# Attention keys in chunks of 128, 128, 128 and 64 instead of 4 x 112, with the rests of scores and values on four quarters of TensorE

## The chip, the cores and the metric

The kernel runs on one core of a Trainium2 chip. The metric is the device time of one launch in microseconds (us). All quoted profiles and all comparisons are of fast runs. A difference of under 2% counts as "same"; where the study needs finer distinctions, the 95% interval of the ratio is given.

## The reference

Eight sequences with twelve heads of 448 tokens and 64 features go through attention with normalised queries and keys; its result, 3584 tokens of 768 features, goes through a normalised feed-forward layer.

```python
B, H, S, D = 8, 12, 448, 64
q_n, k_n = rmsnorm(q, g_q), rmsnorm(k, g_k)
scores = q_n @ k_n.T / sqrt(D)
attn = exp(scores - max) ; attn = attn / (sum(attn) + 1e-9)
x = (attn @ v)  ->  (B*S, H*D)
xn = x / sqrt(mean(x*x) + 1e-6) * rms_g                # 3584 x 768
out = (silu(xn @ w_gate) * (xn @ w_val)) @ w_out       # 768 -> 1536 -> 768
```

The weights arrive as float64 and are turned into fp32 on the chip.

## The kernel before

Heads are worked on in pairs, 48 of them (6 for each sequence). The loop runs over g; iteration g computes the scores of pair g, the values and sums of pair g - 1, and transposes the queries and keys of pair g + 1. The first seven iterations have no feed-forward work to mix in; from then on the feed-forward layer of the sequence before fills TensorE between the attention blocks. With 64 features a head needs half of the array's rows for its scores and half of its columns for its values, so the two heads of a pair run side by side.

Transposed scores: keys on the partitions, 448 queries along the free dimension; four chunks of 112 keys.

```python
def score(g, cs):                       # cs: chunks of keys
    for c in cs:
        for j in range(2):              # the two heads: two row halves of the array
            r = slice(j * D, (j + 1) * D)
            ps = sc[c, j] = ps_s.tile([128, 512], F32, name="sc", tag="s")
            nc.tensor.matmul(ps[0:P, 0:S], lhsT=qkT[r, 1, c * P:(c + 1) * P], rhs=qkT[r, 0, :], start=True, stop=True)
    for (c, j), ps in sc.items():
        e = st["e", g, c, j] = e_pool.tile([P, S], F32, name="e")
        nc.scalar.activation(e, ps[0:P, 0:S], ACT.Exp, scale=rs[:, n:n + 1])
    # ... GpSimd adds the e of one head up into es (late pairs)

def values(g):
    av = st["av", g] = ps_m.tile([128, 512], F32, name="av", tag="m")       # ps_m has one buffer
    for c in range(NT):
        for j in range(2):              # the two heads: two column halves of the array
            nc.tensor.matmul(av[j * D:(j + 1) * D, 0:S], lhsT=vt[:, j, c, :], rhs=st["e", g, c, j],
                             start=(c == 0), stop=(c == NT - 1))

def sums(g):
    # ones times es (late pairs: 2 matmuls) or times every e (the first pairs, "direct": 8 matmuls) -> den
    # rd = 1 / den on VectorE (after a copy on ScalarE in late pairs)
    nc.vector.tensor_tensor(x, av[:, 0:S], rd, ALU.mult)        # frees the bank of av
```

The loop body of the early and of the late iterations (squares, loads and feed-forward calls cut):

```python
if g <= NPAIR:                          # early
    pe(lambda: score(g, (0, 1)))
    ...
    pe(lambda: turn(g + 1, 0)); pe(lambda: turn(g + 1, 1))      # transposes of q and k
    pe(lambda: values(g - 1)); pe(lambda: sums(g - 1))
    pe(lambda: score(g, (2, 3)))
else:                                   # late
    pe(lambda: score(g, (0, 1)))
    pe(lambda: values(g - 1)); pe(lambda: sums(g - 1))
    pe(lambda: score(g, (2, 3)))
    ...                                 # feed-forward work, transposes
```

The conversion of the float64 weights is a pipeline of turns, called a few times an iteration. It shares ScalarE, VectorE and GpSimd with the attention:

```python
def convert():                          # turn n
    if 0 <= n - 4 < len(pieces):        # GpSimd: the last add; frees the raw buffer of piece n - 4
        nc.gpsimd.tensor_tensor(data(key).bitcast(I32), top, lo, ALU.add)
    if 0 <= n - 3 < len(pieces):        # VectorE: three operations
        st["cv", n - 3] = join(*st.pop(("cv", n - 3)))
    if 0 <= n - 2 < len(pieces):        # ScalarE: two operations, the first to read the raw weights
        st["cv", n - 2] = split(st.pop(("raw", n - 2)))
    if n < len(pieces):                 # SyncE: load of piece n, 384 KB, into one of six buffers
        st["raw", n] = load_raw(pieces[n][1])
    if 0 <= n - 6 < len(pieces):
        keep(pieces[n - 6][0])          # SyncE: store of the converted piece
```

## Time and profile before

| | kernel before |
|---|---|
| time, median of 4 runs beside the changed kernel | 1628.51 us (1628.03 to 1629.68) |
| profiled run | 1627.08 us, span 1625.3 us, granted clock 0.999 |
| TensorE, VectorE, ScalarE busy | 99%, 54%, 31% |
| one late pair's attention, start to start | 7.31 us |
| one early pair | 11.32 us |

TensorE is the bound nearly from end to end. The lines that carry this are in the prediction below. In profile lines, L476 and the like are lines of the kernel: before, `sc` is scores, `av` values, `den` sums, `tr` transposes and `ff` the feed-forward layer, all on TensorE (PE).

### The profile page before, as it was taken

The numbers are of one execution on the slowest core, as the hardware profiler recorded it, in microseconds if no ns is written. First come the engines' busy times: TensorE is split into PE (matmuls) and PEld (weight loads), VectorE is DVE, ScalarE is ACT, GpSimd is POOL, SyncE is SP. The second block draws the span as 40 slices with busy tenths as digits, with TensorE's granted clock in tenths as the row PEclk, the third lists the DMA queues.
The fourth block names the chain that finished last, engine by engine and source line by source line (L and its number), as shares of the span: only waits on it lengthen the run. The fifth ranks groups of instructions, "written<-read, shape, count | busy, mean of one in ns | idle before, by whom it ended". The sixth has DMA issues, their size and how long they took to land.

```text
span 1625.3 us, 21571 instructions
## 1 busy us (share of the span) xinstructions
PE 1608.9 (99%) x7376; PEld 1139.7 (70%) x7376; DVE 871.2 (54%) x1425; ACT 500.3 (31%) x975; POOL 632.2 (39%) x569
## 2 busy tenths in 40 slices
PE   8999999999999999999999999999999999999998
PEld 4444445678855888568865788658786588969974
DVE  6989898487842555335572354624565234433431
ACT  7856563232222332232232222322332123100110
POOL 7777776343523434244334323434343223100000
PEclk9999999999999999999999999999999999999999
DMA  8756674666855555565544655466454453557651
GB/s 223 208 176 200 183 219 134 217 222 200 267 183 154 164 154 156 166 197 154 155 120 131 201 155 147 120 215 194 130 163 132 147 176 108 152 182 239 175 148 45
DMA packets 249036, 276.83 MB, mean 170 GB/s; under 512 B 66644, under 2 KB 245844, under 8 KB 248916
## 3 DMA queue, kind: packets, MB, share of 16 engines
q1 hardware_dynamic: 248596, 275.34, 56.7%
q8 instruction: 61, 1.00, 0.3%
q14 instruction: 59, 0.48, 0.1%
q10 hardware_dynamic: 320, 0.00, 0.0%
HBM read 235.93 MB, written 39.32 MB: 169 GB/s over the span
## 4 chain that ended last, share of the span: by engine, by line
PE 91%; DVE 5%; DMA 2%; ACT 1%; issue 0%; POOL 0%; SPq 0%; DVEq 0%; ACTq 0%; POOLq 0%
PE ff L797 41%; PE ff L991 21%; PE sc L476 9%; PE av L501 9%; PE den L512 3%; PE ff L892 3%; PE ff L1022 2%; PE tr L461 2%; DVE top L646 1%; DVE top L645 1%; DVE rd L520 1%; DVE top L644 1%; DMA raw<-in_moe_w_out_dram 0%; ACT e L480 0%; PE rb L558 0%; DMA raw<-in_moe_w_val_dram 0%
## 5 line engine op out<-in xcount | busy, mean ns | idle before, releaser
L797 PE MATMUL ff<-x,w 128*128 128x224 f32 x1770 | 359.3, 353 | 0.8 <-DVE u L809 0.8
L797 PEld LDWEIGHTS ff<-x,w 128*128 128x128 f32 x1770 | 332.2, 190 | 9.8 <-issue 6.7
L797 PE MATMUL ff<-xs,w 128*128 128x224 f32 x1326 | 272.3, 353 | 0.4 <-DVE cc L809 0.4
L480 ACT ACTIVATE e<-sc,rs 112x448 f32<-112x448 f32 x384 | 212.1, 638 | 190.2 <-PE sc L476 185.2
L486 POOL TENSOR_TENSOR es<-e 112x448 f32<-112x448 f32 x82 | 95.3, 1184 | 436.1 <-ACT e L480 436.0
L797 PEld LDWEIGHTS ff<-xs,w 128*128 128x128 f32 x1326 | 248.6, 190 | 6.1 <-issue 5.3
L490 POOL TENSOR_TENSOR es<-es,e 112x448 f32<-112x448 f32 x164 | 185.9, 1144 | 85.4 <-ACT e L480 78.9
L991 PE MATMUL ff<-w,h 128*128 128x384 f32 x600 | 203.4, 488 | 0.0
L520 DVE RECIPROCAL rd<-rd 128x448 f32<-128x448 f32 x41 | 121.1, 2953 | 135.9 <-ACT rd L519 135.9
L476 PE MATMUL sc<-qkT 64*112 64x448 f32 x768 | 176.7, 562 | 1.6 <-DVE qkT L466 0.8
L991 PEld LDWEIGHTS ff<-w,h 128*128 128x128 f32 x600 | 112.3, 190 | 78.6 <-issue 4.7
L501 PE MATMUL av<-e,vt 112*64 112x448 f32 x768 | 154.9, 545 | 0.0
L444 POOL TENSOR_TENSOR rs<-ms,mhalf 112x16 f32<-112x16 f32 (+1 forms) x50 | 143.7, 2874 | 4.2
L476 PEld LDWEIGHTS sc<-qkT 64*112 64x112 f32 x768 | 68.8, 172 | 93.2 <-issue 69.5
L991 PE MATMUL ff<-w,so 128*128 128x384 f32 x338 | 116.7, 488 | 2.0 <-DVE y L952 2.0
L501 PEld LDWEIGHTS av<-e,vt 112*64 112x64 f32 x768 | 50.8, 136 | 95.8 <-issue 73.9
L1022 PE MATMUL ff<-x,w 128*128 128x448 f32 x288 | 112.0, 542 | 0.0
L809 DVE TENSOR_TENSOR cc<-ff,u 128x448 f32<-128x448 f32 x84 | 52.3, 623 | 93.3 <-PE ff L797 93.0
L991 PEld LDWEIGHTS ff<-w,so 128*128 128x128 f32 x338 | 63.2, 190 | 46.5 <-DVE y L952 3.9
L427 DVE TENSOR_REDUCE ms<-sq 112x8 f32<-112x512 f32 x96 | 61.3, 678 | 52.0 <-ACT sq L424 51.7
L682 POOL TENSOR_TENSOR w<-top,raw 128x384 int32<-128x384 int32 x72 | 78.0, 1097 | 28.3 <-DVE top L646 13.4
L1022 PEld LDWEIGHTS ff<-x,w 128*128 128x128 f32 x288 | 53.3, 190 | 50.9 <-issue 49.0
(104 smaller groups left out, 1676.2 us busy)
## 6 DMA issues: line engine op xcount, KB each, us to landing
w<-kept SPq DMA_DIRECT2D x480, 192.0 KB, 3.2
w<-kept_o SPq DMA_DIRECT2D x290, 192.0 KB, 2.8
kept<-w SPq DMA_DIRECT2D x94, 192.0 KB, 3.7
top<-kept SPq DMA_DIRECT2D x72, 192.0 KB, 3.0
qk<-in_q_dram SPq DMA_DIRECT2D x48, 224.0 KB, 3.6
qk<-in_k_dram SPq DMA_DIRECT2D x96, 112.0 KB, 3.5
vt<-in_v_dram SPq DMA_DIRECT2D x48, 224.0 KB, 2.8
raw<-in_moe_w_gate_dram SPq DMA_DIRECT2D x24, 384.0 KB, 4.7
```

Of the source, the lines that this page charges most:

```text
L427: nc.vector.tensor_reduce(out=ms[:, i * n:(i + 1) * n], in_=sq.rearrange("p (n d) -> p n d", d=D), axis=AX_X, op=ALU.add)
L444: nc.gpsimd.tensor_tensor(st["rs", g][:, cols], ms, mhalf[0:P, cols], ALU.pow)
L476: nc.tensor.matmul(ps[0:P, 0:S], lhsT=qkT[r, 1, c * P:(c + 1) * P], rhs=qkT[r, 0, :], start=True, stop=True)
L480: nc.scalar.activation(e, ps[0:P, 0:S], ACT.Exp, scale=rs[:, n:n + 1])
L486: nc.gpsimd.tensor_tensor(es, st["e", g, 0, j], st["e", g, 1, j], ALU.add)
L490: nc.gpsimd.tensor_tensor(es, es, st["e", g, c, j], ALU.add)
L501: nc.tensor.matmul(av[j * D:(j + 1) * D, 0:S], lhsT=vt[:, j, c, :], rhs=st["e", g, c, j], start=(c == 0), stop=(c == NT - 1))
L520: nc.vector.reciprocal(rd, rd)
L682: nc.gpsimd.tensor_tensor(data(key).bitcast(I32), top, lo, ALU.add)
L797: nc.tensor.matmul(bank[:, w * HT:(w + 1) * HT], lhsT=wt[:, c * 128:(c + 1) * 128], rhs=x[:, c, :], start=onto is None and w == c == 0, st ...
L991: nc.tensor.matmul(ps, lhsT=a, rhs=data(("wo", b, name, c)), start=first and c == 0, stop=c == NFP - 1, skip_group_check=True)
L1022: nc.tensor.matmul(bank[w][:, 0:S], lhsT=data(key)[:, c * 128:(c + 1) * 128], rhs=st["x", 0, half][:, c, :], start=half == c == 0, stop=ha ...
```

## The change

Its intent: 448 is three and a half times 128. With chunks of 112 keys the array's 128 columns (scores) or rows (values) are used to seven eighths, four times. With 3 x 128 + 64, three slots are full; the rest of 64 keys needs only a quarter of the array for each matmul (64 rows, 64 columns), so two heads' score rests (the two diagonal quarters) and two heads' value rests of the pair before (the other two) could run in one slot. For that the features of the two heads trade places in x (`place(j)`), and the feed-forward weights' rows are loaded in the matching order. The core of the diff:

```diff
-        for h in range(2):
-            nc.sync.dma_start(out=qk[:, 1]...[:, h], in_=k[b, 2 * hp + h]...)        # and q in one transfer
+        nc.sync.dma_start(out=to[:, :, 0:NK * D], in_=q[b, hs, full]...)             # 6 transfers a pair in place of 3
+        nc.sync.dma_start(out=to[0:REST, :, NK * D:], in_=q[b, hs, rest]...)         # 32 KB
+        for h in range(2):
+            nc.sync.dma_start(out=to[:, h, 0:NK], in_=k[b, 2 * hp + h, full]...)
+        nc.sync.dma_start(out=to[0:REST, :, NK], in_=k[b, hs, rest]...)              # 32 KB
+        nc.sync.dma_start(out=to[REST:128, 0, NK], in_=k[b, 2 * hp + 1, rest])       # 16 KB
 # values: 3 transfers in place of 1
+    def place(j):
+        return slice((1 - j) * D, (2 - j) * D)
+    def rests(g):
+        part = [slice(j * REST, (j + 1) * REST) for j in range(2)]
+        for r in part:                                          # scores of pair g, diagonal quarters
+            nc.tensor.matmul(ps[r, 0:S], lhsT=qkT[r, 1, NK * 128:S], rhs=qkT[r, 0, :], ...)
+        av = st["av", g - 1] = ps_m.tile([128, 512], F32, name="av", tag="m")
+        for j, r in enumerate(part):                            # values of pair g - 1, the other two quarters
+            nc.tensor.matmul(av[place(j), 0:S], lhsT=vt[r, 2 * NK * D:], rhs=e[r, :], start=True, stop=False, ...)
+        if direct(g - 1):                                       # early pairs: rests of the sums as well
+            ...
+        nc.scalar.activation(e, ps[:, 0:S], ACT.Exp, ...)       # one exponential for both heads' rests
 # the loop, early and late
-            pe(lambda: score(g, (0, 1)))
+        pe(lambda: (rests(g), score(g, (0,)) if g < NG else None))
 ...
-            pe(lambda: score(g, (2, 3)))
+            pe(lambda: score(g, (1, 2)))
 # raw weights: two pieces at a time, three double buffers for six single ones
-    raw_pool, cv_pool = pool("c_raw", 6), pool("c_cv", 4)
+    raw_pool, cv_pool = pool("c_raw", 3), pool("c_cv", 4)
-        if n < len(pieces):
-            st["raw", n] = load_raw(pieces[n][1])
+        if n < len(pieces) and n % 2 == 0:
+            load_raw(n)
```

Why the weights are paired: the swapped rows make a gate or value piece two transfers (64 partitions each). Pairing two pieces keeps the number of transfers as it was. Cut: the memsets of the padding, 128 for 112 in normalisation and transposes, and the output's rows.

## The prediction

> **What bounds the kernel now.** I read the engine table first, then the stretch table (busy time of each engine in chosen windows), then the time line of TensorE in one late pair and in one early pair, and last the chain of waits at the start.
>
> ```profile
> PE 1608.9 (99%) x7376; PEld 1139.7 (70%) x7376; DVE 871.2 (54%) x1425; ACT 500.3 (31%) x975; POOL 632.2 (39%) x569
> 55.00:65.00 10.00, 10.00 (x52) 4.21 (x50) 9.79 (x13) 7.76 (x16) 7.73 (x7) 1.00 0.76 231
> 600.00:1000.00 400.00, 399.35 (x1918) 299.46 (x1917) 187.14 (x309) 113.02 (x218) 151.18 (x135) 1.00 0.54 159
> ```
>
> TensorE is busy 99% of 1625.3 us, at full granted clock (1.00), with VectorE at half load from 600 us on. So an array slot saved there is time saved. Early (55 to 65 us) VectorE is at 98% as well; that stretch has to be read by itself.
>
> One pair of heads with the feed-forward work around it (columns: start, duration, operation, count of records):
>
> ```profile
> 622.23 1.76 PE L476 MATMUL sc<-qkT 64*112 64x448 f32 x8
> 623.92 3.23 PE L501 MATMUL av<-e,vt 112*64 112x448 f32 x16
> 626.98 0.92 PE L512 MATMUL den<-es,ones 112*64 112x448 f32 x4
> 627.83 1.78 PE L476 MATMUL sc<-qkT 64*112 64x448 f32 x8
> 629.54 2.54 PE L797 MATMUL ff<-x,w 128*128 128x224 f32 x12
> 605.44 0.55 PE L461 MATMUL tr<-ident,qn 112*128 112x112 f32 x4
> 605.83 2.45 PE L797 MATMUL ff<-x,w 128*128 128x224 f32 x12
> ```
>
> An fp32 matmul leaves two records, so these are 4, 8, 2 and 4 matmuls. From start to start: scores 1.69, values 3.06, sums 0.85, scores 1.71; together 7.31 us. Inside a block the records start in twos about 7 ns apart and the next two follow 0.376 us later: the two matmuls of a slot, on two halves of the array, run at once, each in two passes of 0.376. A **slot** thus costs 0.75 us and holds two half-array matmuls. A change of the array's division shows at a block's edges: the first pass takes 0.467 (scores) or 0.427 (values), the last one before another division 0.472. That is 0.15 to 0.19 us per change of division.
>
> The early pairs (the first six of batch 0, whose sums go straight through TensorE with 8 matmuls):
>
> ```profile
> 47.64 4.30 PE L476 MATMUL sc<-qkT 64*112 64x448 f32 x16
> 51.88 0.60 PE L461 MATMUL tr<-ident,qn 112*128 112x112 f32 x4
> 52.31 0.55 PE L461 MATMUL tr<-ident,qk 112*128 112x112 f32 x4
> 52.79 3.23 PE L501 MATMUL av<-e,vt 112*64 112x448 f32 x16
> 55.85 3.18 PE L512 MATMUL den<-e,ones 112*64 112x448 f32 x16
> 47.83 2.96 DVE L516 RECIPROCAL rd<-den 128x448 f32<-128x448 f32 x1 [0.29 <-PE den L512]
> 50.82 0.62 DVE L527 TENSOR_TENSOR x<-av,rd 128x448 f32<-128x448 f32 x1
> ```
>
> A pair takes 58.96 - 47.64 = 11.32 us. The bank of the values (one buffer) is read by the product of L527, which ends 51.44, that is 3.8 us after the sums ended. Today the next values start at 52.79, behind eight scores and the transposes: the wait is hidden.
>
> The start is a chain through the DMA queue; its piece that ends last is the third pair's keys:
>
> ```profile
> 6.26 0.57 SPq L400
> 6.83 0.04 issue
> 6.88 3.60 DMA qk<-in_k_dram
> 10.47 0.02 issue
> ```
>
> **What the Trainium skill says.** (1) "TensorEngine Tiling (Array Packing)", Tiling Modes: 64x64 gives four independent tiles, and changing the mode drains TensorE. The trace agrees on the drain (0.15 to 0.19 us above) and shows two tiles at once; it has no four. (2) "TensorE: Matmul & The Clock Gate", Part 3, gives a pack's span as one matmul plus about 4 ns per further tile; here the second starts 7 ns later, as cheap. (3) "PSUM — Partial Sum Buffer", on collisions: matmuls of different row tiles may not write one bank and quadrant together. In the change each group of columns writes two different banks (scores' rest and values' rest), so nothing forbids the overlap. (4) "DMA: Bandwidth & Descriptors" puts a fixed cost of about 2 us on every transfer; the trace has 2.8 to 3.6 us to landing for queries, keys and values. Splitting them adds issues, not only bytes.
>
> **The change, part by part.**
>
> *Late pairs (iterations 8 to 47, 40 of them).* The keys go 3 x 128 + 64 in place of 4 x 112, so scores and values need 3 slots each in place of 4, and the two rests share one slot: scores on the diagonal quarters, values of the pair before on the other two (that is why heads are swapped in x). New blocks: rests 0.467 + 0.47 = 0.94; scores of chunk 0 0.94; values 0.427 + 5 x 0.376 = 2.31; sums 0.85; scores of chunks 1 and 2 1.71. Sum 6.75 against 7.31: **0.56 saved** (one slot of 0.75 less one more change of division, 0.19). Against it: transposes stream 128 columns in place of 112. They start 0.096 us apart for 112, so 0.110 for 128; eight of them cost 0.11 more. Net 0.45 us a pair, 40 x 0.45 = **18.0 us**. Nothing else holds these pairs: ScalarE loses one of eight exponentials, GpSimd keeps three adds per head (later, but 20 us ahead of their use), and the last bank of scores still waits for the copy of the sums as now.
>
> *Early pairs (iterations 2 to 7).* The values' rest now stands *before* the pair's first scores. Its bank is the one that L527 has still to read. Let T be the end of the sums. Scores of chunks 1 and 2 end at T + 1.7, the scores' rest can run, but the values' rest must wait until about T + 3.9 (0.2 + 2.96 + 0.62 and semaphores). Then values' and sums' rests, which lie on the same quarters, 1.69: T + 5.6; scores of chunk 0, 6.5; transposes 1.05, 7.6; values 2.31, 9.9; six sums' matmuls 2.35, **12.25** against 11.32. Six iterations x 0.93 = **5.6 us lost**. Iteration 1 has no predecessor to wait for and gains 0.6; the last iteration, 48, loses 0.2.
>
> *Start.* A pair's queries and keys are 6 transfers in place of 3, values 3 in place of 1. Ahead of the first exponentials ScalarE squares three pairs in order, so the third pair's keys bound it. They were the 10th issue, now the 21st. At 0.3 to 0.6 us an issue (0.39 for a query, 0.57 to 0.7 for a head of keys, less for rests, my estimate) 21 issues take about 9.0 us where ten took 5.7 to 6.3: **3.3 us lost**. The memsets of the padding (VectorE, idle then) are hidden.
>
> *Weights.* Loaded two pieces at a time with the same bytes; three double buffers for six single ones. ScalarE needs a piece two turns after its load was issued (7 us; landing 4.3 to 4.7 us). I count nothing.
>
> Sum: 1628.4 - 18.0 - 0.6 + 0.2 + 5.6 + 3.3 = 1618.9; I say **1618**.
>
> **The rivals.** (a) *No four at once*: if the values' rests follow the scores' rests, each late pair pays two more passes, 0.75: 40 x 0.75 = 30 us, total about 1648. For it: no four-way overlap is in this trace, and a pass could be bound by reading two streams from the same 64 partitions. Against it: the values already read two streams from the same 112 partitions at full pace. I give it 10%. (b) *The early wait is not there* or hides behind other work: 1612 to 1613; with no start cost either, 1609, the floor. Against it: one buffer, and a reciprocal of 2.96 us that nothing else covers. (c) *The DMA queue becomes a bound early*: about 15 transfers a pair in place of 10 or 11, issued in order, and weight loads wait for GpSimd one turn longer than before. If ScalarE starves on raw weights, PE waits 1 to 2 us more a pair: 1625 to 1632. Against it: the DMA share is 0.76 early, and the pair lasts longer.
>
> **Range and chances.** The 18 us of the late pairs are the firmest term (1 us either way, outside rival a). Early and start terms together may be 2 to 20 us. So 1604 to 1634 should hold it 8 times in 10. Faster by over 2% means under 1596, below the floor of 1609: 3%. Slower by over 2% means over 1661, above even rival (a) alone: 3%. Within 2%: 94%.
>
> **What would show each step right or wrong.** Late pair: blocks of about 0.94, 0.94, 2.31, 0.85 and 1.71 us; eight records of the two rests starting in fours. If the rest block takes 1.7 us, rival (a) holds. Early pairs: an idle of TensorE of 1.2 to 2.2 us before the values' rest, released by VectorE's x, and a cadence near 12.2 us. Start: the first exponentials near 14.5 us in place of 11.1. Late transposes 0.11 us apart. The prediction is wrong if late pairs gain under 0.3 us, or if TensorE's waits in the first 100 us are on ScalarE or a DMA rather than on x.

## The result and the profile after

The changed kernel took **1648.34 us** (median of 4, 1647.18 to 1649.76) against 1628.51 us, ratio 1.0121 with a 95% interval of 1.0104 to 1.0139. (A ratio here is the mean time of one kernel's fast runs over that of the other's of the same rounds, so not quite the ratio of the medians.) The predicted 1618 us was wrong in sign, and the result lies above the range of 1604 to 1634; the class "within 2%" was right. That 1648 is also the figure of rival (a) is a coincidence, as the next lines show.

The engine table of the changed kernel: TensorE is less busy than before (1601.5 for 1608.9 us), but the span is 22 us longer.

```profile
PE 1601.5 (97%) x7376; PEld 1131.8 (69%) x7376; DVE 880.7 (53%) x1433; ACT 478.8 (29%) x927; POOL 637.2 (39%) x569
```

**A late pair** of the changed kernel, time line of TensorE (start, duration, operation, count of records); L521 and L526 are the rests of scores and of values.

```profile
623.31 0.59 PE L521 MATMUL sc<-qkT 64*64 64x448 f32 x2
623.32 0.59 PE L526 MATMUL av<-e,vt 64*64 64x448 f32 x2
623.73 0.54 PE L521 MATMUL sc<-qkT 64*64 64x448 f32 x2
623.75 0.54 PE L526 MATMUL av<-e,vt 64*64 64x448 f32 x2
624.22 1.02 PE L491 MATMUL sc<-qkT 64*128 64x448 f32 x4
625.17 2.48 PE L544 MATMUL av<-e,vt 128*64 128x448 f32 x12
627.48 0.92 PE L557 MATMUL den<-es,ones 128*64 128x448 f32 x4
628.33 1.80 PE L491 MATMUL sc<-qkT 64*128 64x448 f32 x8
630.06 1.40 PE L850 MATMUL ff<-x,w 128*128 128x224 f32 x6
```

Two scores' and two values' records start within 0.02 us of each other, the second passes follow 0.42 us later: four at once. Start to start the blocks take 0.91, 0.95, 2.31, 0.85 and 1.73 us, 6.75 in sum, which is the predicted sum. Rival (a) is dead already: its rest block would take 1.7 us.

**An early pair** of the changed kernel: first VectorE's reciprocal and product (which frees the values' bank), then TensorE. The bracket says how long the engine had been idle and what ended that; "issue" means that the profile shows no releaser.

```profile
46.51 2.95 DVE L561 RECIPROCAL rd<-den 128x448 f32<-128x448 f32 x1
49.49 0.62 DVE L572 TENSOR_TENSOR x<-av,rd 128x448 f32<-128x448 f32 x1
```

```profile
47.33 0.97 PE L521 MATMUL sc<-qkT 64*64 64x448 f32 x4 [2.43 <-ACT e L495]
50.22 1.76 PE L526 MATMUL av<-e,vt 64*64 64x448 f32 x4 [1.92 <-issue]
51.73 1.73 PE L531 MATMUL den<-e,ones 64*64 64x448 f32 x4
...
60.03 1.77 PE L491 MATMUL sc<-qkT 64*128 64x448 f32 x8
...
63.93 0.97 PE L526 MATMUL av<-e,vt 64*64 64x448 f32 x4 [1.19 <-issue]
...
72.22 1.77 PE L491 MATMUL sc<-qkT 64*128 64x448 f32 x8
```

The values' rest starts at 50.22, 0.11 us after the product ended at 50.11: the predicted wait is there, for x, although the profile names no releaser. From 60.03 to 72.22 a pair takes 12.19 us (predicted 12.25). But at 47.33 TensorE had already waited 2.43 us for an exponential of ScalarE: not predicted, and one of the signs that the prediction had named against itself. (Of TensorE's waits in the first 100 us, 8.1 us are still for x and 2.9 us for exponentials.) And the two blocks after it are 1.76 and 1.73 us long; the same blocks of the next pair take 0.97 and 0.95. The stretch table of the same run says why: the columns end with the granted clock, the DMA share and GB/s, and the clock had fallen to half.

```profile
50.00:53.00 3.00, 2.78 (x8) 0.84 (x8) 2.86 (x8) 0.24 (x1) 2.06 (x3) 0.50 1.08 287
```

The Trainium skill, "TensorE: Matmul & The Clock Gate", Part 1, says that TensorE's clock drops to half after an idle stretch; this agrees, with a clock of 0.50 after 4.35 us of idle time around a block of 0.97 us. It was not the only time, as the next part shows.

**Where the time goes.** The first transpose of each pair's queries is a marker that both kernels have. The lag of the changed kernel behind the one before, in us, at marker 2 (in iteration 1), 8 (in iteration 7) and so on, differenced:

| stretch | predicted | changed kernel |
|---|---|---|
| start to marker 2 (iterations 0 and 1) | +2.7 | +4.96 |
| marker 2 to 8 (iterations 2 to 7, early pairs) | +5.6 | +11.45 |
| 8 to 13 (weights are still being converted) | -2.25 | **+18.68** |
| 13 to 19 | -2.7 | +1.34 |
| 19 to 47 (28 late pairs) | -12.6 | -13.85 |
| 47 to the end | -0.25 | -0.20 |
| sum | -9.5 | +22.38 |

The last 28 pairs gain 0.49 us each (predicted 0.45). Most of the miss is between markers 8 and 13, which are 102 to 240 us into the kernel before and 119 to 275 us into the changed one. Two stretch lines from there, before and after (columns: the stretch, its length, busy time of PE, PEld, DVE, ACT and POOL, then clock, DMA share and GB/s):

```profile
125.00:300.00 175.00, 173.36 (x616) 85.83 (x615) 146.87 (x198) 89.14 (x177) 122.84 (x106) 1.00 0.62 187
```

```profile
125.00:300.00 175.00, 160.46 (x546) 76.75 (x546) 147.06 (x201) 83.76 (x169) 121.20 (x101) 0.96 0.65 180
```

TensorE stands idle, and its clock is below full. Between the markers it is idle for 14.5 us (before: 1.6) and runs at half clock four times for 3.41 us, each fall coming 0.7 to 1.1 us after the end of a wait of 2.3 to 4.1 us; before, never. So the loss of 18.68 us here has two parts: the waits, and slower matmuls after them.

What TensorE waits for there is exponentials of ScalarE (14.3 us, five times). ScalarE's own wait table tells why they are late (columns: engine, operation, line; waited for; us in total, times, longest us; of the whole run). Before:

```profile
ACT top L638 <- DMA raw<-in_moe_w_val_dram: 5.7, 3, 2.5
...
ACT top L638 <- DMA raw<-in_moe_w_out_dram: 4.1, 4, 1.6
...
ACT top L638 <- DMA raw<-in_moe_w_gate_dram: 1.2, 1, 1.2
```

After:

```profile
ACT top L692 <- DMA raw<-in_moe_w_out_dram: 27.8, 9, 4.7
...
ACT top L692 <- DMA raw<-in_moe_w_gate_dram: 22.9, 7, 7.3
...
ACT top L692 <- DMA raw<-in_moe_w_val_dram: 16.2, 4, 5.2
```

ScalarE waits 66.9 us for raw weights instead of 11.0. One such wait, followed through the changed kernel's time line of all engines (SPq is SyncE's queue of transfers; L735 is GpSimd's last add of the conversion, which frees a raw buffer):

```profile
183.28 0.56 DVE L700 SCALAR_TENSOR_TENSOR top<-raw,top 128x384 int32<-128x384 int32 x1
...
185.40 3.00 POOL L459 TENSOR_TENSOR rs<-ms,mhalf 128x16 f32<-128x16 f32 x1
...
186.52 0.57 ACT L692 ACTIVATE top<-raw 128x384 f32<-128x384 f32 x1 [3.60 <-DMA raw<-in_moe_w_gate_dram]
...
189.61 4.47 POOL L735 TENSOR_TENSOR w<-top,raw 128x384 int32<-128x384 int32 x4
...
190.95 1.28 SPq L682 DMA_DIRECT2D raw<-in_moe_w_val_dram  x2
...
197.23 0.56 ACT L692 ACTIVATE top<-raw 128x384 f32<-128x384 f32 x1 [5.25 <-DMA raw<-in_moe_w_val_dram]
...
202.84 3.77 PE L491 MATMUL sc<-qkT 64*128 64x448 f32 x8 [4.13 <-ACT e L536]
```

The loads of two value pieces are issued at 190.95, as soon as the first of GpSimd's four adds from 189.61 on is done (190.93); the second lands 6.2 us later, at 197.12; ScalarE has by then stood 5.25 us. The exponentials of the scores stand in ScalarE's queue behind that conversion and two more, so TensorE waits 4.13 us for them; its eight records from 202.84 then take 3.77 us where a late pair's take 1.80, in part because the clock is at half from 203.52 on. The add that freed the buffer had had its input since 183.84, the end of VectorE's L700; GpSimd first worked through the norms of a later pair (185.11 to 189.64, L459 among them). The last of the four adds converts the piece for which ScalarE had waited until 186.52; it ends at 194.07, and the next pair's load is issued at 194.25. So every delay of an add is now a delay of a load, and a late load makes a later one late.

A count of turns explains it. A piece is loaded in turn n and its buffer is freed by the add in turn n + 4. Six single buffers: the load of turn n + 6 reuses that buffer, with a whole turn between. Three double buffers: the second piece of a pair is freed in turn n + 5, and the load of turn n + 6, the very next, needs the buffer. The memory is the same, one turn of slack is gone. This is theory A; it is tested first. (Its rival, theory B of the expectations below, is that the many small transfers of queries, keys and values delay the weights in the one queue.)

### The profile page after: what moved, and what is told of

Read it like the earlier page. It is cut to its first block, busy times and chain, and to the rows that moved or that the text cites. A ratio compares the mean times of both kernels' runs of the same rounds, so it can differ in the third digit from the quotient of the medians.

```text
span 1647.7 us, 21690 instructions
## 1 busy us (share of the span) xinstructions
PE 1601.5 (97%) x7376; PEld 1131.8 (69%) x7376; DVE 880.7 (53%) x1433; ACT 478.8 (29%) x927; POOL 637.2 (39%) x569
## 4 chain that ended last, share of the span: by engine, by line
PE 84%; DVE 5%; DMA 4%; SPq 2%; POOL 2%; ACT 2%; issue 1%; POOLq 0%; ACTq 0%; DVEq 0%
PE ff L850 39%; PE ff L1051 21%; PE sc L491 7%; PE av L544 6%; PE ff L948 3%; PE den L557 2%; PE sc L521 2%; PE tr L476 2%; DMA raw<-in_moe_w_out_dram 1%; PE ff L1082 1%; DVE top L700 1%; DMA raw<-in_moe_w_gate_dram 1%; DVE top L699 1%; POOL w L735 1%; DMA raw<-in_moe_w_val_dram 1%
## 5 line engine op out<-in xcount | busy, mean ns | idle before, releaser
L502 POOL TENSOR_TENSOR es<-e 128x448 f32<-128x448 f32 x82 | 95.9, 1169 | 586.6 <-ACT e L495 586.6
L495 ACT ACTIVATE e<-sc,rs 128x448 f32<-128x448 f32 x288 | 162.7, 635 | 41.6 <-PE sc L491 40.4
L491 PE MATMUL sc<-qkT 64*128 64x448 f32 x576 | 145.2, 593 | 14.5 <-ACT e L536 14.3
L459 POOL TENSOR_TENSOR rs<-ms,mhalf 128x16 f32<-128x16 f32 (+1 forms) x50 | 143.4, 2867 | 4.2
L491 PEld LDWEIGHTS sc<-qkT 64*128 64x128 f32 x576 | 56.7, 190 | 99.8 <-issue 72.3
L544 PE MATMUL av<-e,vt 128*64 128x448 f32 x576 | 118.8, 548 | 0.0
L503 POOL TENSOR_TENSOR es<-es,e 128x448 f32<-128x448 f32 x82 | 94.4, 1151 | 8.4 <-ACT e L495 2.2
L504 POOL TENSOR_TENSOR es<-es,e 64x448 f32<-64x448 f32 x82 | 94.8, 1156 | 6.4
L442 DVE TENSOR_REDUCE ms<-sq 128x8 f32<-128x512 f32 x96 | 61.4, 677 | 60.0 <-ACT sq L439 60.0
L735 POOL TENSOR_TENSOR w<-top,raw 128x384 int32<-128x384 int32 x72 | 78.4, 1105 | 24.2 <-DVE top L700 12.7
```

Of the source, the lines that this page charges most:

```text
L459: nc.gpsimd.tensor_tensor(st["rs", g][:, cols], ms, mhalf[:, cols], ALU.pow)
L491: nc.tensor.matmul(ps[:, 0:S], lhsT=qkT[r, 1, c * 128:(c + 1) * 128], rhs=qkT[r, 0, :], start=True, stop=True)
L495: nc.scalar.activation(e, ps[:, 0:S], ACT.Exp, scale=rs[:, n:n + 1])
L502: nc.gpsimd.tensor_tensor(es, st["e", g, 0, j], st["e", g, 1, j], ALU.add)
L503: nc.gpsimd.tensor_tensor(es, es, st["e", g, 2, j], ALU.add)
L504: nc.gpsimd.tensor_tensor(es[r], es[r], rest[r], ALU.add)
```

## The experiments

The rival explanations were: the values' rests standing early (the prediction's own early term), the start's longer queue of transfers, and (for completeness) the four quarters. Every kernel below gave correct outputs. "Ratio" is to the kernel before.

### 1. The kernel before with nothing but the paired weights

```diff
-    raw_pool, cv_pool = pool("c_raw", 6), pool("c_cv", 4)
+    raw_pool, cv_pool = pool("c_raw", 3), pool("c_cv", 4)
-        raw = raw_pool.tile([128, 2 * BW], I32, name="raw")
+        raw = raw_pool.tile([128, 2, 2 * BW], I32, name="raw")      # two pieces, one transfer
-        if n < len(pieces):
+        if n < len(pieces) and n % 2 == 0:
```

> The kernel before with one part of the change alone: raw weights loaded two pieces at a time into three double buffers, one transfer for both (no heads swapped, no other edit). Theory A (the double buffers take the slack out of the weight conversion: a pair of pieces is in use for six turns, and three double buffers hold exactly six): this alone costs 14 to 25 us, 1643 to 1653 us, with ScalarE waiting on raw weights in the stretch of 100 to 260 us and TensorE behind it. Theory B (it is the many small transfers of queries, keys and values that delay the weights in the one DMA queue): 1628 us, within 3 us of the kernel before.

Measured: 1644.63 us (1644.24 to 1646.25), ratio 1.0102 [1.0085, 1.0119]. The old kernel with this one part loses 16 us. Its lag is +0.67 up to marker 8 and +16.86 at marker 13, and it stays there: the loss is made in the same stretch as in the changed kernel (+16.19 against +18.68). ScalarE's wait table of this run, two of its lines:

```profile
ACT top L641 <- DMA raw<-in_moe_w_out_dram: 25.6, 9, 4.3
...
ACT top L641 <- DMA raw<-in_moe_w_val_dram: 14.0, 4, 5.1
```

Theory A's prediction came true (14 to 25 us), with nothing of the attention changed; theory B, which expected 1628 us, is out. (Here one transfer carries two pieces, not two halves; so it is the pairing, not the splitting by partitions.) In this run too TensorE's clock is at half for 13.65 us between markers 8 and 13.

### 2. The changed kernel with a fourth double buffer

```diff
-    e_pool, tmp, y_pool = pool("c_e", 12), pool("c_tmp", 1), pool("c_y", 2)
+    e_pool, tmp, y_pool = pool("c_e", 10), pool("c_tmp", 1), pool("c_y", 2)
-    raw_pool, cv_pool = pool("c_raw", 3), pool("c_cv", 4)
+    raw_pool, cv_pool = pool("c_raw", 4), pool("c_cv", 4)
```

(and three buffers for `es` in place of four, to make room)

> The changed kernel with four double buffers of raw weights in place of three (room made by ten exponential buffers in place of twelve and three of sums in place of four). Theory A: iterations 8 to 13, which lose 19 us against the kernel before, lose at most 3, and the early iterations 2 and 3 get back 3 to 5 of their 9: 1624 to 1629 us. Theory B: no more than 3 us faster than the changed kernel, 1645 to 1648 us.

Measured: 1632.35 us, ratio 1.0021 [1.0004, 1.0038]. Between markers 8 and 13 the lag grows by 1.76 instead of 18.68 us, as theory A expected, and at the end it is 5.83. The transfers are the same, so bytes, DMA share and issue count were not what hurt there: the missing slack was. But the other half of the expectation failed: the time lies above 1624 to 1629 us, and the early pairs (markers 2 to 8) get back only 1.0 us (10.42 for 11.45). What raw weights cost there is not a matter of slack.

### 3. The changed kernel with single weights

Six single buffers and the old list of pieces again; because of the swapped rows, a gate or value piece is two transfers of 64 partitions.

```diff
-        if n < len(pieces) and n % 2 == 0:
+        if n < len(pieces):
+            # one piece into one of six buffers
+            for j in range(2):
+                nc.sync.dma_start(out=to[place(j)], in_=src[j * D:(j + 1) * D])
```

> The changed kernel with raw weights loaded one piece at a time into six single buffers as before; because heads are swapped, a piece of the gate and value weights takes two half transfers, so there are 60 more transfers in the queue than in the changed kernel. Theory A: 1622 to 1630 us, the weight waits of iterations 8 to 13 gone. Theory B: no better than the changed kernel, 1648 us or more, for the queue gets longer.

Measured: 1630.62 us, ratio 1.0011 [0.9994, 1.0029]. From marker 8 to 13 the lag now grows by 1.27 instead of 18.68. The whole of it falls from 22.38 to 3.05: the pairing cost **19.3 us** of the changed kernel. Of these, 17.4 us fall between markers 8 and 13: some 10.5 us less idle time of TensorE, and some 6.9 us less busy time (134.4 us for 141.3). In this run the clock stays full there; 13.65 us at half clock, all of them busy, would account for 6.8 us. Another 4.1 us fall in the early pairs; the start takes 1.8 us back. The time is 0.6 us above the expected range. The predicted gain does not come out either: 1618.9 was the sum without any cost of weights.

### 4. The changed kernel without the swap of heads

```diff
     def place(j):
-        return slice((1 - j) * D, (2 - j) * D)
+        return slice(j * D, (j + 1) * D)
```

Now the values' rests lie on the same quarters as the scores' rests.

> The changed kernel without the swap of heads: the rest of the values lies on the same two quarters as the rest of the scores, so the two follow each other. It measures what four quarters at once are worth. If they truly run at once: the rest block of a late pair grows from 0.91 to about 1.66 us, 40 late pairs lose 0.75 us each, 30 us, about 1678 us (early pairs nearly unchanged). If the overlap is an artefact of the records: within 5 us of the changed kernel.

Measured: 1673.01 us (1672.77 to 1673.56), ratio 1.0274 [1.0257, 1.0291], the only kernel of the study that is slower by over 2%. Time line of TensorE, the rest block of a late pair:

```profile
661.35 0.97 PE L521 MATMUL sc<-qkT 64*64 64x448 f32 x4
662.15 0.92 PE L526 MATMUL av<-e,vt 64*64 64x448 f32 x4
```

The two rests run one after the other: the block takes 1.65 us (the next starts at 663.00) in place of 0.91, and the lag rises by 0.24 us in each of the last 28 pairs, where the changed kernel's falls by 0.49. The swap is worth 0.74 us a pair: one slot, as the prediction's rival (a) priced it. This is also the direct proof that four quarters run at once in the changed kernel. (The whole kernel loses 23 us of lag by it, 24.7 by the medians, not the 30 us expected for 40 pairs: where TensorE is not the only bound, a longer block costs less.)

### 5. Early values' rests behind the transposes

On top of 3: for the early pairs the rests of values and sums are issued together with the other values, after the transposes, where they stood before the change.

```diff
 def rests(g):
-        if g:
-            # rests of values (and of sums, if direct)
+        if g and not direct(g - 1):
+            value_rests(g - 1)
 def values(g):
+        if direct(g):
+            value_rests(g)
```

> On top of the kernel with single weight pieces (1630.6 us): in the early pairs alone, whose sums go straight through TensorE, the rests of values and sums are issued with the values, after the transposes, and no longer ahead of the pair's first scores. Theory (they wait there for the one bank of values that VectorE has still to read): the six waits of 1.1 to 1.9 us before the values' rest go, an early pair takes 11.4 to 11.7 us in place of 12.3, and the kernel gains 3 to 5 us, 1625 to 1628 us. Rival (the early pairs are bound by VectorE, 98% busy, or by weights, and the wait only shows it): the wait moves to another instruction and the time stays within 1 us of 1630.6.

Measured: 1627.76 us, ratio 1.0003 [0.9987, 1.002]. The six waits for x are gone from TensorE's wait table (one of 1.1 us is left on that line's successor). Part of them moved: between 20 and 120 us TensorE now waits 2.7 us for exponentials and 2.3 us for normalised queries (run 3: at most 0.8 for both). Between markers 2 and 8 the lag grows by 4.25 instead of 7.39 us. So the early place of the rests costs 3 to 4.5 us (3.1 by this difference, 4.5 if one stops at marker 7, as the lag wanders by a microsecond or two), somewhat under the 5.6 predicted; the total falls by 3.3 (from a lag of 3.05 at the end to -0.23). This rests on one profile of each kernel: by the times the gain over run 3 is not shown, since the ratios of 1.0011 and 1.0003 differ by 1.3 us and their intervals overlap.

### 6. Scores of chunk 0 ahead of the rests

On top of 3, another way to hide the same wait, at no cost in division changes:

```diff
-        pe(lambda: (rests(g), score(g, (0,)) if g < NG else None))
+        pe(lambda: (score(g, (0,)) if g < NG else None, rests(g)))
```

> On top of the kernel with single weight pieces (1630.6 us): the pair's first scores (chunk 0) are issued ahead of the block of rests in place of after it, everywhere. It keeps four quarters at once and puts one slot of work into the wait for the bank. Theory: the six early waits shrink by 0.9 us each and one change of division goes, 4 to 6 us gained, 1625 to 1627 us; late pairs unchanged at 6.75 us. Rival as for the run before: no gain.

Measured: 1629.59 us, ratio 1.0011 [0.9995, 1.0028]: less than expected, and no gain over run 3 by the ratio. TensorE's wait table of run 3, then of this one:

```profile
PE av L526 <- issue: 8.4, 6, 1.9
PE sc L491 <- ACT e L536: 3.4, 3, 2.1
```

```profile
PE sc L491 <- ACT e L495: 6.9, 6, 2.0
...
PE av L526 <- PE sc L521: 2.1, 3, 0.8
```

The values' rest waits 2.1 us instead of 8.4, but now the scores in front of it wait for ScalarE's exponentials: 2.6 of the 6.9 us are in the early pairs, where run 3 had no such wait, and 4.4 come later (run 3: 3.4). From marker 2 to 8 the lag grows by 5.83 us instead of 7.39.

### 7. and 8. The start: gains first, and all together

In the changed kernel ScalarE issues four small loads of the gains between 1.90 and 6.29 us, and its first squares, queued behind them, start at 6.34 (before: 4.01). On top of 3, these loads are issued before everything else (7), and then with 6 and with the third pair's loads ahead of the first values (8):

```diff
+    gq = const.tile([128, 1], F32, name="gq")          # and gk: four loads on ScalarE
     for g in range(2):
         load_pair(g)
 # (8) also
-    load_v(0)
     load_pair(2)
+    load_v(0)
```

> On top of the kernel with single weight pieces (1630.6 us): ScalarE's four small loads of gains are issued ahead of the loads of the first pairs. [...]in the changed kernel ScalarE issues the gains between 1.9 and 6.3 us, waiting each time, and only then squares the first queries. Theory: the first squares move from 6.3 to about 4.0 us and the first transposes of queries come 2.3 us earlier; the third pair's keys still come late (the queue has 21 transfers before), so the end gains 0 to 2.3 us: 1628 to 1631 us. If all of the start's 5 us were due to the gains: 1625.6 us.

Measured: 1630.96 us, ratio 1.002 [1.0003, 1.0037]. The first squares start at 4.69 and marker 0 gets 1.7 us back (+0.66 for +2.35), marker 1 gets none (+6.30 for +6.20): the gains were in front of the first squares, but the third pair's keys bind the next step, as expected.

> Single weight pieces, first scores ahead of rests, gains first, and the third pair's queries and keys loaded ahead of the first values (18 transfers before its last keys in place of 21). Theory, by sum from 1630.6: less 5, less 2, less 1: 1621 to 1625 us, faster than the kernel before by 0.2 to 0.5%. If the parts do not add up (each waits for the next limit): 1625 to 1629 us.

Measured: 1627.98 us, ratio 1.0001 [0.9984, 1.0017]. The parts do not add up: the lag is +3.38 at marker 2 and +8.43 at marker 3. With the start shorter, the early pairs run into weights and exponentials that are not there yet (TensorE waits 10.7 us for exponentials in this run). Its profiled run, at 1631.70 us, is the slowest of its four, so these lags are not typical of the kernel. Which transfer's delay is to blame was not isolated.

### 9. and 10. The small transfers from another queue

The start in the profile: the last key issue of the third pair and the first exponential, kernel before and then changed kernel (SPq: SyncE's queue; duration is the time that the issue takes).

```profile
6.26 1.24 SPq L400 DMA_DIRECT2D qk<-in_k_dram  x2
...
11.11 3.24 ACT L480 ACTIVATE e<-sc,rs 112x448 f32<-112x448 f32 x6
```

```profile
10.44 0.59 SPq L407 DMA_DIRECT2D qk<-in_q_dram  x1
...
11.07 0.62 SPq L408 DMA_DIRECT2D qk<-in_q_dram  x1
...
13.72 0.60 SPq L413 DMA_DIRECT2D qk<-in_k_dram  x1
...
16.30 0.62 ACT L536 ACTIVATE e<-sc,rs 128x448 f32<-128x448 f32 x1
```

An issue of 192 KB (L407) takes 0.59 us here, one of 32 KB (L408) 0.62, one of 16 KB (L413) 0.60: a small rest costs as much of the queue as a large load. Over the whole run it costs more: the medians of 48 issues each are 0.39, 0.63 and 0.60 us. The prediction had guessed "less for rests". So on top of 5, the three rests of queries and keys of pairs 1 and 2 go through GpSimd's queue (9), and then those of pairs 1 to 9 and the values' rests of pairs 0 to 9 (10):

```diff
+        queue = nc.gpsimd if 0 < g < 3 else nc.sync
-        nc.sync.dma_start(out=to[0:REST, :, NK * D:], ...)
+        queue.dma_start(out=to[0:REST, :, NK * D:], ...)         # and the two rests of keys
```

> On top of the kernel with single pieces and late values (1627.8 us): the rests of queries and keys of the second and third pair (six small transfers) are issued by GpSimd and no longer by the one queue that issues the rest. Theory (the start is bound by the number of transfers that this queue issues, about 0.62 us each whatever their size): the third pair's keys are issued some 3.7 us earlier, iteration 2 starts 3 to 4 us later than in the kernel before in place of 6.3, and the kernel gains 1 to 3 us, 1625 to 1627 us. Rival (the start is bound by the bytes or by ScalarE): no gain, or a loss where GpSimd's issue delays its own work on the norms.

Measured: **1624.18 us** (1622.16 to 1625.63), ratio 0.9976 [0.996, 0.9993]. Marker 2 comes 1.5 us earlier than in 5 (+4.83 for +6.34), and markers 2 to 8 lose 1.81 instead of 4.25. The second profile of the same kernel, in run 11, repeats the latter (1.70) but not the former (+5.86), so what the start itself gained is not settled; expected were 3 to 4 us at iteration 2.

> The same, for the rests of queries, keys and values of the first ten pairs. Theory: the queue, which issues back to back from 16 to 55 us, gets gaps, and the waits for raw weights at iterations 2 to 4 shrink as well: another 1 to 3 us, 1623 to 1626 us. Rival: GpSimd, busy three quarters of the early stretch, becomes the bound; its issues cost more than they free, 1628 us or more.

Measured: 1630.64 us, ratio 1.0015 [0.9999, 1.0032]. Too much of it: GpSimd also normalises the queries, and TensorE now waits for it. Its longest entry in TensorE's wait table of this run:

```profile
PE tr L477 <- POOL qn L464: 6.4, 6, 1.9
```

The Trainium skill, "DMA: Bandwidth & Descriptors", section "Issuing engines are not separate DMA queues", says that issuing from several engines saves only the sequencer's time to issue. Run 9 fits: six issues of about 0.6 us left SyncE's queue and about 3 us were gained against run 5 (the lag at the end falls from -0.23 to -3.02). Run 10 shows the other side: the time is spent on the engine that issues instead.

### 11. The best version again

The same kernel as in 9, in five rounds.

> The fastest version so far once more (single raw buffers, the early values' rests behind the transposes, the rests of the second and third pair's keys and queries issued by GpSimd), word for word the same kernel, in five rounds for a narrower interval. If its gain is real: 1622 to 1626 us against 1628, ratio 0.996 to 0.999 with an interval that stays below 1. If the first measurement was luck: a ratio of 0.999 to 1.001.

Measured: 1624.30 us (1623.19 to 1627.30, 5 runs) against 1629.0, ratio 0.9972 [0.9958, 0.9985]. The gain over the kernel before is small but real: about 0.3%, or 4.6 us by the ratio.

### The stretches side by side

Change of lag behind the kernel before, in us, from the profiled runs:

| stretch (markers) | predicted | changed | 1: before, paired | 3: single | 5: values late | 9: rests by GpSimd |
|---|---|---|---|---|---|---|
| start to 2 | +2.7 | +4.96 | +0.67 | +6.77 | +6.34 | +4.83 |
| 2 to 8 | +5.6 | +11.45 | 0.00 | +7.39 | +4.25 | +1.81 |
| 8 to 13 | -2.25 | +18.68 | +16.19 | +1.27 | +1.36 | +2.45 |
| 13 to 19 | -2.7 | +1.34 | 0.00 | +1.65 | +1.66 | +1.66 |
| 19 to 47 | -12.6 | -13.85 | -0.29 | -13.84 | -13.86 | -13.85 |
| 47 to end | -0.25 | -0.20 | -0.06 | -0.19 | +0.02 | +0.08 |
| sum | -9.5 | +22.38 | +16.51 | +3.05 | -0.23 | -3.02 |

## Why the prediction was wrong

- **Late pairs: right.** Each block came out within 0.03 us, the sum of 6.75 us exactly; the net gain is 0.49 us a pair for 0.45. The size of the term was off in another way: "40 x 0.45 = 18.0" took every late pair to be bound by TensorE. Up to marker 13 TensorE is not the only bound, even with single weights (+1.27 instead of -2.25 there), so only the last 28 pairs hand their gain on in full.
- **Weights: the step that failed.** The prediction's words: "ScalarE needs a piece two turns after its load was issued (7 us; landing 4.3 to 4.7 us). I count nothing." It compared the landing with the turns until the data are needed, and left out when a load can be issued at all: when a buffer is free. Run 1 puts 16 us on this one part, runs 2 and 3 take 16.6 and 19.3 us of it back (lag at the end). About 7 of the 17 us between markers 8 and 13 are not the waits themselves but the half clock that follows them, of which the prediction had no term. The failed step is rival (c) in its own mechanism ("weight loads wait for GpSimd one turn longer than before", "ScalarE starves on raw weights"), which the prediction named and then sized too small (1625 to 1632) and weighed too lightly. The argument used against it, a DMA share of 0.76, was beside the point: in the changed kernel that share is 0.65 between 125 and 300 us and ScalarE starves all the same.
- **Early pairs: right mechanism, one of several.** The wait for x came as predicted (1.2 to 2.3 us, cadence 12.19 for 12.25). The measured cost of the rests' early place is 3 to 4.5 us for 5.6. The stretch lost 11.45 us because ScalarE also waited for raw weights there (about 4 us, changed kernel against run 3; a fourth buffer gave back only 1.0 of them, so the cause is not the slack and stays open) and because of the queue of small transfers (2.4 us, run 5 against run 9). TensorE's clock fell to half once in these pairs: some 1.6 us (two blocks of 1.7 for 0.95), in part the same microseconds.
- **Start: right mechanism, too small.** The first exponential came at 16.30 us (predicted 14.5, before 11.11), the third pair's last key issue at 13.72 (predicted 9.0, before about 6.9). The mis-sized term is the issue: 0.6 us for every transfer of the start, whatever its size, and the estimate had "less for rests".
- **Rival (a): refuted** by the starts within 0.02 us and by run 4, which is what (a) would have looked like: 1.65 us, as it said.
- **Rival (b): refuted.** The early wait was there six times.
- **Open.** Between markers 17 and 19 every kernel with the new chunks loses 2.5 us (4.0 without the swap): TensorE waits for VectorE's sum u in the feed-forward layer for 3.3 us in all, where the kernel before waits 0.8. No run told why. Also open is why markers 8 to 13 do not gain even with single weights (TensorE idles 4.1 us there for 1.6 before, 3.4 of them for ScalarE's exponentials), and why the parts of run 8 did not add up.

## What to carry to other kernels

Count buffers in turns, not in bytes: pairing the loads of a ring keeps memory, bytes and transfers equal and still takes away the turn of slack that hid a load's flight, and this cost more (16 to 17 us, of 19 for the pairing in all) than the change's core gained (about 14 us in the pairs where it counts). A wait of TensorE can cost more than its length, because the matmuls after it may run at half clock: here about 7 us on top of 10. A blocked in-order engine passes its wait to whoever is queued behind: here raw weights stopped exponentials, and these TensorE. Splitting a tensor into full chunks and a rest pays on the array, but each rest is a transfer that costs a full issue; put those on an engine with spare time where a start is bound by the queue, and only those.

## What the Trainium skill lacked or had wrong

- "DMA: Bandwidth & Descriptors", on the anatomy of a transfer and on issuing engines: about 50 ns for the sequencer's dispatch (given for transfers that GpSimd issues), and the time to initiate a transfer is called usually small. No time measured on this chip stands there for an issue in SyncE's queue (the nearest is a count of sequencer cycles for "previous generations", in the part on trn3). In the start of the changed kernel an issue took 0.6 us for 16, 32 and 192 KB alike (medians of the whole run: 0.60, 0.63 and 0.39), against 2.1 to 2.9 us (medians) from issue to landing of the small rests; 21 such issues set the end of the start.
- "TensorEngine Tiling (Array Packing)", Tiling Modes: it has no price for a change of mode; 0.15 to 0.19 us each here. What it says of four independent 64x64 tiles holds: 0.91 us for four matmuls, 1.65 us when two pairs share quarters.
- No page: how many turns of slack a ring of buffers needs when loads are paired. Three buffers of two pieces in place of six of one cost 16 us here, with the same bytes.
